# Block-sparse attention by query blocks of 32, 256 score columns a head, in front of a decoded-weight MLP

## The chip, the cores and the metric

The kernel runs on one core of one Trainium2 chip. The time is device microseconds of one execution. TensorE multiplies (PE in the profile, PEld its weight loads), VectorE (DVE), ScalarE (ACT) and GpSimd (POOL) do the element-wise work, and SyncE (SP) issues the transfers to 16 DMA engines.

## The reference

Attention over 4 batches, 8 heads, 768 positions and 64 dimensions, in blocks of 32; then a two-layer MLP on the 3,072 tokens of 512 features.

```python
scores = scale * np.matmul(q, k.transpose(0, 1, 3, 2))
mask = np.abs(blk_i - blk_j) <= window          # window = 1, blocks of 32, 24 of them
mask = mask | (blk_i == 0) | (blk_j == 0) | (blk_i == n_blocks - 1) | (blk_j == n_blocks - 1)
for qb in range(n_blocks):
    for kb in sampled_blocks[qb]:               # 3 drawn blocks per query block
        mask[qb * block:(qb + 1) * block, kb * block:(kb + 1) * block] = True
scores = np.where(mask, scores, -1000000000.0)
attn = np.exp(scores - np.max(scores, axis=-1, keepdims=True))
attn = attn / (np.sum(attn, axis=-1, keepdims=True) + 1e-09)
x = np.matmul(attn, v)                          # then [tokens, 512]
h = x @ w_in                                    # 512 x 2048
r = np.maximum(h, 0.0)
out = (s * (r * r) + b) @ w_out                 # 2048 x 512
```

So a query of an inner block sees its own block and both neighbours, the first and the last block, and three drawn ones: eight blocks, 256 keys, some of which coincide and are masked out. The queries of the first and of the last block see all 768 keys. q and k are 8 times larger than the draw above would give. The weights arrive as 64-bit floats.

## The kernel before

The attention part is cut into 52 slots, 26 for each pair of batches (pair 0 is batches a and b of the ORD strings, L26-33). Of the 26, 20 are s slots: 128 queries (four inner blocks, t = 0 to 4) of four heads (x = 0 or 1) of one batch. Two are h slots (t = 5, the remaining two inner blocks of all eight heads, packed as four units of 128 rows), and four are d slots, the dense queries of the first and last block. In pair 0 the d slots come first, in pair 1 last.

A slot's work goes through these steps. Its scores go to PSUM, one head per bank: `scores_static` (L878) multiplies 128 queries by 256 keys, which are six neighbouring blocks (own and neighbour blocks of all four query blocks) and the two outer blocks, read from `k_seq`, a layout of K that holds the outer blocks again between the others. `scores_sampled` (L904) adds 96 columns for the three drawn blocks of each query block, in tiles of 64 x 32, from `kg`, into which GpSimd copies the drawn blocks (L838). VectorE adds the mask and finds the maximum over 352 columns (L919), ScalarE exponentiates (L931), TensorE transposes three pieces of 128 x 128 per head (L955), and VectorE or ScalarE copies them out (L959, L961), one copy per head. TensorE then multiplies by the values: `av_static` (L1000) two pieces of 128 keys by 64 columns, from `v_sta`, and `av_sampled` (L1014) the drawn ones from `vg`, which is filled block by block by indexed loads on SyncE's queue (L821). The result is scaled (L1020), transposed (L1026), copied (L1031) and written to a scratch tensor in DRAM, `xd` (L1043). The result and its transpose live in one PSUM bank of their own, so a slot's values begin when the slot before has been copied out. d slots have their own code (L892 scores, L989 values).

Weights: each 128 x 512 block of `w_in` (i0 to i15) and `w_out` (o0 to o15) is loaded raw (L57) and turned by `decode_f64` into a high and a low part, on VectorE in six steps (L75, L77, L78, L83, L84, L85) and ScalarE in three. The MLP of batch 0 then runs as a first layer `mlp1` (L404-406: high x high, high x low, low x high), relu (L409), square (L416), high and low part of the hidden values (L420, L421, L425), and a second layer `mlp2` (L446-448). Its input is read back from `xd` (L364) and split into two parts (L377 on ScalarE, L379 on VectorE). The later batches use sums of blocks in seven products (L583).

The order on every engine is fixed before the run by the class `Plan`, a list scheduler: each operation has an engine, a modelled cost, a due number counted in units (heads), what it depends on and which rotating buffer it takes. At each step the operation that can start first by the model is put next on its engine. TensorE's attention order is tied by hand: transposes of slot i, the transpose of x of slot i-1, scores of slot i+2, values of slot i. The table T (L26-33) holds how many units ahead loads stand (KL for K, GK for the copies of drawn keys, GV for drawn values, VL for values), and the order of the decodes (WL).

Of the kernel before, what the change touches and what calls it, by code (L numbers as in the profile page):

```python
# [9 lines left out]
F32 = mybir.dt.float32  # L10
F32R = mybir.dt.float32r
# [191 lines left out]
def kernel(  # L203
# [26 lines left out]
    KW = k_seq.shape[-1]  # L230
    SC = 256
    SW = SC + NSL * BLK
# [23 lines left out]
    def kbig(q, name):  # L256
        return kp.tile([P, NPAIR, KW], F32R, tag=f"kt{q}", name=name, bufs=1)

# [9 lines left out]
    gp = ctx.enter_context(tc.tile_pool(name="gp", bufs=4))  # L268
# [25 lines left out]
    def win(f, part):  # L294

        return win_tile(f // 4)[:, (4 * part + f % 4) * NW:(4 * part + f % 4 + 1) * NW]

    def win_tile(k):
        if k not in wts:
            wts[k] = kbig(k, f"win{k}").rearrange("p a c -> p (a c)")  # L300
        return wts[k]
# [58 lines left out]
    xsp, xraw = {}, {}  # L360
# [6 lines left out]
    def xsplit(g, c, part=None):  # L367
# [5 lines left out]
        for k in range(2) if part is None else (part,):  # L373
            if c == 0:
                xsp[(g, k)] = gp.tile([P, NCC, HALF], F32R, tag="kg", name=f"x{g}_{k}")
# [108 lines left out]
    def ready_rest():  # L484
# [3 lines left out]
        spare = [win_tile(k)[:, 8 * NW:8 * NW + HN] for k in range(4)]  # L488
# [29 lines left out]
    def xplace(n):  # L518
        if n not in xop:
            t = gp.tile([P, 2 * HX], F32R, tag="kg", name=f"x{n}")  # L520
            xop[n] = t[:, :HX], t[:, HX:]
        return xop[n]
# [104 lines left out]
    with ExitStack() as es:  # L627
# [3 lines left out]
        vp = es.enter_context(tc.tile_pool(name="vp", bufs=4))  # L631
# [23 lines left out]
        def load_k(b, p):  # L655
            if p == 0:
                kts[b] = kbig(b, f"kt{b}").bitcast(F32)
            nc.sync.dma_start(out=kts[b][:, p, :], in_=k_seq[b, p])

        qraw, vst = {}, {}  # L660
# [10 lines left out]
        def load_v(i, pr):  # L671
            kind, b, t, x = slots[i]
            vt = vp.tile([P, NCH, P], F32, tag="v", name=f"v{i}_{pr}")
            if kind == "d":
                h0 = (2 * x + pr) * P
                nc.sync.dma_start(out=vt, in_=v[b, :, h0:h0 + P].rearrange("(c p) d -> p c d", p=P))
            elif kind == "h":
                vt = vt.rearrange("p c d -> p (c d)")[:, :8 * D]
                nc.sync.dma_start(out=vt.rearrange("p (x d) -> p x d", x=2), in_=v_edge[b].rearrange("x p d -> p x d"))
            else:  # L680
                vt = vt.rearrange("p c d -> p (c d)")[:, :8 * D].rearrange("p (c d) -> p c d", c=2)
                nc.sync.dma_start(out=vt, in_=v_sta[b, t, x])
            vst[(i, pr)] = vt

# [9 lines left out]
        for t in ptiles:  # L694
            nc.gpsimd.memset(t[:, SW:], 0.0)

# [26 lines left out]
        def sampled_blocks():  # L723
# [3 lines left out]
        mh = pers.tile([P, 2 * P], BF16, name="mh")  # L727
        kidx = pers.tile([P, (4 * NSP + 2) * NSL], I32, name="kidx")
        vidx = pers.tile([P, (4 * NSP + 2) * NSL], I32, name="vidx")


        wm = pers.tile([P, 6], F32, name="wm")
        V.tensor_scalar(out=wm, in0=jf[:, :6], scalar1=rf, scalar2=-1.0, op0=ALU.subtract, op1=ALU.add)
        V.tensor_tensor(out=wm, in0=wm, in1=wm, op=ALU.mult)
        V.tensor_scalar(out=wm, in0=wm, scalar1=1.0, scalar2=NEG, op0=ALU.is_gt, op1=ALU.mult)
        nc.gpsimd.memset(ms[:, :, P:P + 2 * BLK], 0.0)
        nc.scalar.copy(ms[:, :, :P].rearrange("p t (c e) -> p t c e", e=BLK),
                       wm[:, :4].unsqueeze(1).unsqueeze(3).broadcast_to([P, NSP, 4, BLK]))
        nc.scalar.copy(ms[:, :, P + 2 * BLK:SC].rearrange("p t (c e) -> p t c e", e=BLK),
# [715 lines left out]
```

## Time and profile before

| what | value |
|---|---|
| median of three runs | 802.29 us (799.03 to 805.81) |
| the profiled execution, its span | 803.1 us |
| first score matmul (a d slot) | 11.2 us |
| values of the first s slot | 47.75 us |
| last copy of transposed weights / last values of attention | 281.4 / 283.4 us |
| first matmul of the second layer | 297.6 us |

The profile is of one execution of 803.1 us, 0.1% above the median. Engine shares are shares of that span. In the rows of a stretch, busy time of each engine stands with the number of instructions in brackets, then the clock that TensorE was granted (1.00 is full speed), the busy share of the 16 DMA engines, and GB/s. In rows of time the first number is the start, the second the duration, x the number of instructions in a row; fp32 matmuls leave two records each. The bracket at the end gives idle time ahead and what ended it.

### The profile page before, as it was taken

The page shows a single profiled execution, that of the slowest core. Times are in us where ns is not written, and L with a number is a line of the kernel's source. Part 1 is how long each engine was busy: PE and PEld are TensorE (multiplying, and loading weights), DVE is VectorE, ACT ScalarE, POOL GpSimd, SP SyncE. Part 2 cuts the span into 40 slices and gives each one's busy share as a digit, 9 for nine tenths or more (in the row PEclk, how much of TensorE's full clock was granted, in tenths as well). Part 3 has the DMA queues.
Part 4 walks back from the last instruction along what each step waited for, and adds up shares of the span by engine and source line. Part 5 has one row for each costly group of instructions (what it writes and reads, how often), then busy time and mean ns, then how long its engine had stood idle before and what let it go on. Part 6 is the DMA issues. An engine that isn't in the chain of part 4 may idle for free.

```text
span 803.1 us, 22021 instructions
## 1 busy us (share of the span) xinstructions
PE 777.3 (97%) x8352; PEld 674.1 (84%) x8352; DVE 606.0 (75%) x1528; ACT 501.7 (62%) x1190; POOL 178.2 (22%) x404
## 2 busy tenths in 40 slices
PE   7898999899999999999998999999999999999997
PEld 6587877788877798999987999998888988999986
DVE  5476768788888898998789678678667768766662
ACT  3576768688787877778875443467355457544542
POOL 5422124222400000000003322233223223222321
PEclk9899999999999999999999999999999999999999
DMA  9998898877778532544332222024000012000002
GB/s 251 244 233 306 222 260 221 252 199 210 207 218 267 167 112 79 184 158 131 131 118 93 79 101 91 27 86 156 3 0 1 1 40 98 1 1 1 1 0 79
DMA packets 89001, 100.99 MB, mean 126 GB/s; under 512 B 11584, under 2 KB 66368, under 8 KB 88896
## 3 DMA queue, kind: packets, MB, share of 16 engines
q1 hardware_dynamic: 88896, 99.59, 41.2%
q8 instruction: 66, 1.08, 0.6%
q14 instruction: 39, 0.32, 0.1%
HBM read 80.68 MB, written 14.68 MB: 119 GB/s over the span
## 4 chain that ended last, share of the span: by engine, by line
PE 83%; DVE 5%; DMA 4%; ACT 3%; SPq 2%; issue 2%; ACTq 0%; DVEq 0%
PE m L583 19%; PE o L447 10%; PE o L448 10%; PE o L446 10%; PE t L955 8%; PE xs L1000 5%; PE s L878 5%; PE xs L1014 3%; PE h L404 3%; PE h L406 3%; PE h L405 3%; DMA kt<-in_k_seq_dram 2%; PE s L904 2%; PE xs L989 1%; PE s L892 1%
## 5 line engine op out<-in xcount | busy, mean ns | idle before, releaser
L425 POOL TENSOR_TENSOR hid<-hid,hid 128x384 fp32r<-128x384 f32 x96 | 106.1, 1106 | 468.5 <-ACT hid L601 457.3
L600 ACT ACTIVATE hid<-hid,sb_b,sb_s 128x384 f32<-128x384 f32 x96 | 68.0, 709 | 151.7 <-DVE hid L594 151.6
L931 ACT ACTIVATE ptile<-ptile,nm 128x352 f32<-128x352 f32 (+2 forms) x208 | 121.0, 584 | 33.8 <-DVE nm L919 33.2
L919 DVE CUSTOM_DVE_ANT_0 ptile<-s,ms 128x352 f32<-128x352 f32 x160 | 74.3, 521 | 29.0 <-PE s L904 28.5
L838 POOL COPY kg<-kt 128x128 f32 x264 | 64.1, 297 | 138.8 <-PE s L904 126.2
L955 PE MATMUL t<-ident,ptile 128*128 128x128 f32 x608 | 80.0, 281 | 4.7 <-ACT ptile L931 3.1
L583 PE MATMUL m<-wout,win 128*128 128x384 f32 x384 | 83.5, 338 | 1.0 <-ACT xrest L1348 1.0
L448 PE MATMUL o<-woutr,hid 128*128 128x512 f32 x192 | 75.9, 395 | 0.0
L447 PE MATMUL o<-woutr,hid 128*128 128x512 f32 x192 | 75.8, 395 | 0.0
L955 PEld LDWEIGHTS t<-ident,ptile 128*128 128x128 f32 x608 | 66.7, 142 | 10.5 <-ACT ptile L931 4.0
L446 PE MATMUL o<-woutr,hid 128*128 128x512 f32 x192 | 74.6, 389 | 0.0
L583 PEld LDWEIGHTS m<-wout,win 128*128 128x128 f32 x384 | 68.9, 188 | 4.9 <-ACT xrest L1348 1.4
L959 DVE COPY pt<-t 128x384 f32<-128x384 f32 (+1 forms) x104 | 56.2, 544 | 8.9 <-PE t L955 7.1
L961 ACT COPY pt<-t 128x384 f32<-128x384 f32 (+1 forms) x104 | 48.3, 474 | 17.6 <-PE t L955 16.7
L583 PE MATMUL m<-xT,wop 128*128 128x384 f32 x288 | 58.3, 337 | 0.0
L594 DVE SCALAR_TENSOR_TENSOR hid<-hid 128x384 f32<-128x384 f32 x96 | 54.5, 568 | 3.3
L601 ACT CAST hid<-hid 128x384 fp32r<-128x384 f32 x96 | 49.3, 514 | 7.8 <-PE o L448 0.4
L583 PEld LDWEIGHTS m<-xT,wop 128*128 128x128 f32 x288 | 51.5, 188 | 2.1
L593 DVE TENSOR_TENSOR hid<-m,xrest 128x384 f32<-128x384 f32 x48 | 26.5, 552 | 30.2 <-issue 25.6
L1000 PE MATMUL xs<-v,pt 128*64 128x64 f32 x1280 | 46.5, 225 | 2.1 <-issue 2.1
L1000 PEld LDWEIGHTS xs<-v,pt 128*64 128x64 f32 x1280 | 40.7, 138 | 9.0 <-issue 2.3
L448 PE MATMUL o<-wout,hid 128*128 128x512 f32 x120 | 47.4, 395 | 0.0
(186 smaller groups left out, 1759.6 us busy)
## 6 DMA issues: line engine op xcount, KB each, us to landing
vg<-in_v_dram SPq DMA_DIRECT2D x136, 128.0 KB, 3.6
v<-in_v_sta_dram SPq DMA_DIRECT2D x40, 256.0 KB, 4.4
kt<-in_k_seq_dram SPq DMA_DIRECT2D x16, 544.0 KB, 8.1
raw_i<-in_w_in_dram SPq DMA_DIRECT2D x16, 512.0 KB, 4.9
raw_o<-in_w_out_dram SPq DMA_DIRECT2D x16, 512.0 KB, 3.3
v<-in_v_dram SPq DMA_DIRECT2D x16, 384.0 KB, 7.1
xd<-xst SPq DMA_DIRECT2D x44, 128.0 KB, 3.4
out_dram<-ob SPq DMA_DIRECT2D x20, 256.0 KB, 2.0
```

Source lines behind the costliest of these rows:

```text
L425: (eng or nc.vector).tensor_tensor(out=htile(5 + i % 3), in0=t, in1=gh.bitcast(F32), op=ALU.subtract)
L446: nc.tensor.matmul(acc, gh[:, tsl], wout(f, 0), start=first, stop=False)
L447: nc.tensor.matmul(acc, gh[:, tsl], wout(f, 1), start=False, stop=False)
L448: nc.tensor.matmul(acc, gl[:, tsl], wout(f, 0), start=False, stop=last)
L583: nc.tensor.matmul(to, w_, x_, start=(c == 0 and k == 0), stop=(c == 1 and k == 2))
L600: nc.scalar.activation(t, t, AF.Identity, bias=sb_b, scale=sb_s)
L838: nc.gpsimd.tensor_copy(kg[:, m], kts[b][:, :, bass.ds(box["js"][m], BLK)])
L919: nc.vector.tensor_tensor_reduce(out=pt[:, :w], in0=sps.pop((n, g))[:, :w], in1=msk, scale=-scale, scalar=FMAX if g == 0 else nm[:, 0:1], ...
L931: nc.scalar.activation(pt[:, :w], pt[:, :w], AF.Exp, bias=nms[n][:, last:last + 1], scale=-1.0, accum_out=dns[i][:, g, j:j + 1])
L955: nc.tensor.transpose(tp[:, c, :], src[:, c * P:(c + 1) * P], ident)
L959: nc.vector.tensor_copy(to, src)
L1000: nc.tensor.matmul(xs[rows], pt[:, c, rows], vt[:, c, hp * D:(hp + 1) * D], start=(j == 0 and c == 0), stop=False, skip_group_check=True)
```

## The change

Every inner query block now gets its own eight blocks of keys and nothing more: 256 score columns for each head instead of 352. The columns are the own block and its neighbours (0 to 95, `OWN`), one outer block (96 to 127), the three drawn blocks (128 to 223, `SAM`), the other outer block (224 to 255). All scores of s and h slots come from `scores_piece`, in tiles of 64 x 32 (one per query block, head and piece); both kinds of slot run the same code. Values come from `av` in tiles of 128 x 32, with 128 keys each: the own window with the first block, and the drawn blocks with the last block. Two heads share a PSUM bank, in the scores (two banks a slot instead of four) and in the transposes (four pieces of 128 x 128 in a bank, copied out together, one copy on VectorE and one on ScalarE).

For this K is loaded by pairs of batches from `k_blk`, block by block, in four parts of 786,432 bytes, and any score of the pair waits for all four. `kg` holds the drawn keys of both batches (two buffers instead of four, each twice as large; half as many copies, twice as wide). The values of an s slot are loaded as windows: for each of its four query blocks the 96 rows around it, from `v`, into one of four fixed places `vw` (by batch of the pair and x), whose last 32 rows hold the first block, loaded once for a batch and half. `vg` gets the last block in its last 32 rows. The buffers for values of d and h slots fall from four to three. Decoded `w_in` blocks lie in other places (six in each K tile, four in the `vw` places). The split x lies in the `kg` buffers. Three masks and an index table are no longer built. In T, GK goes from 9 to 13, VL from 10 to 12, and KL has one entry for each pair.

```diff
-    "GK": 9.0, "GV": [9.0, 15.0, 15.0, 15.0, 15.0, 15.0], "KL": [26.0, 18.0, 26.0, 26.0], "QL": 18.0, "VL": 10.0, "SI": -30.0, "MS1": -30.0, "MS2": -29.0,
+    "GK": 13.0, "GV": [9.0, 15.0, 15.0, 15.0, 15.0, 15.0], "KL": [26.0, 40.0], "QL": 18.0, "VL": 12.0, "SI": -30.0, "MS1": -30.0, "MS2": -29.0,
...
-    SC = 256
-    SW = SC + NSL * BLK
+    SW = 256
+    OWN, SAM = 0, 4 * BLK
...
-    gp = ctx.enter_context(tc.tile_pool(name="gp", bufs=4))
+    gp = ctx.enter_context(tc.tile_pool(name="gp", bufs=2))
...
-        return win_tile(f // 4)[:, (4 * part + f % 4) * NW:(4 * part + f % 4 + 1) * NW]
+        k, n = (f // 6, 2 * (f % 6) + part) if f < 12 else (f - 10, part)
+        return win_tile(k)[:, n * NW:(n + 1) * NW]
...
-        vp = es.enter_context(tc.tile_pool(name="vp", bufs=4))
+        vp = es.enter_context(tc.tile_pool(name="vp", bufs=3))
...
-            nc.sync.dma_start(out=kts[b][:, p, :], in_=k_seq[b, p])
+            rows = slice(part * NB // KP, (part + 1) * NB // KP)
+            nc.sync.dma_start(out=kts[e][:, rows].rearrange("p n a c -> p n (a c)"),
+                              in_=k_blk[rows, :, 2 * e:2 * e + 2, :].rearrange("n p a c -> p n (a c)"))
...
-                nc.sync.dma_start(out=vt, in_=v_sta[b, t, x])
+                vt = window_place(b, x)
+                nc.sync.dma_start(out=vt[:NSL * BLK], in_=window_rows(b, 4 * t, 4, x * DM // 2, DM // 2))
...
+        def window_rows(b, first, n, d0, nd):
+            return bass.AP(v.tensor, v.offset + (b * S + first * BLK) * DM + d0, [[DM, NSL * BLK], [BLK * DM, n], [1, nd]])
...
+        def load_first_block(b, x):
+            nc.sync.dma_start(out=window_place(b, x)[NSL * BLK:],
+                              in_=v[b, :BLK, x * DM // 2:(x + 1) * DM // 2].unsqueeze(1).broadcast_to([BLK, 4, DM // 2]))
...
-                nc.gpsimd.tensor_copy(kg[:, m], kts[b][:, :, bass.ds(box["js"][m], BLK)])
+                nc.gpsimd.tensor_copy(kg[:, m:m + 1].rearrange("p o a c -> p o (a c)"),
+                                      kts[e][:, bass.ds(box["js"][m], 1)].rearrange("p o a c -> p o (a c)"))
...
+        def scores_piece(i, k, keys_of, o, n, two=False):
+            qr, u = qraw[slots[i][:3]], unit_of[i]
+            for par in range(2):
+                to = sps[(u + 2 * k + par, 0)][:, o:o + n]
+                if two:
+                    to = sps[(u + 2 * k + par, 0)].rearrange("p (a c) -> p a c", a=2)[:, :, o:o + n]
+                for r in range(4):
+                    pair, m, block = part_of(i, k, r)
+                    rows = slice(r * BLK, (r + 1) * BLK)
+                    nc.tensor.matmul(to[rows], qr[halves[par], pair, rows], keys_of(halves[par], pair, m, block),
+                                     start=True, stop=True, tile_position=(par * D, r * BLK))
...
+            scores_piece(i, k, lambda rows, pair, m, block: keys(b, rows, slice(block - 1, block + 2), pair), OWN, NSL * BLK)
+            scores_piece(i, k, lambda rows, pair, m, block: keys(b, rows, slice(0, NB, NB - 1), pair), NSL * BLK, BLK, True)
...
+            for j in range(1 if dense else 2):
+                src = pbuf[(n + j, g)]
+                for c in range(3 if dense else 2):
+                    nc.tensor.transpose(tp[:, (2 * j + c) * P:(2 * j + c + 1) * P], src[:, c * P:(c + 1) * P], ident)
...
+                    values = vg[:, b % 2, m, (h0 + h) * D:(h0 + h + 1) * D] if c else own[:, m, h * D:(h + 1) * D]
+                    nc.tensor.matmul(xs[rows], pt[:, c, rows], values, start=(j == 0 and c == 0), stop=(c == 1),
                                      tile_position=(0, r * BLK), skip_group_check=True)
```

What this makes of TensorE's rows in one s slot of batch 0, from its scores to its neighbour's values. Before (xs is the result, pt the transposed weights, x4 four matmuls alike):

```order
L878 MATMUL s_2663<-kt_184,qr_3s 128x256
L878 MATMUL s_2665<-kt_184,qr_3s 128x256
L878 MATMUL s_2675<-kt_184,qr_3s 128x256
L878 MATMUL s_2677<-kt_184,qr_3s 128x256
L904 MATMUL s_2663<-kg_3_1651,qr_3s 32x96 x4
L904 MATMUL s_2665<-kg_3_1651,qr_3s 32x96 x4
L904 MATMUL s_2675<-kg_3_1651,qr_3s 32x96 x4
L904 MATMUL s_2677<-kg_3_1651,qr_3s 32x96 x4
L1000 MATMUL xs_2702<-v_0_2238,pt_0_2657 64x64 x4
```

And in the new order, on the same engine at the same place (the first and second row are the own blocks, the third and fourth the outer ones):

```order
L920 MATMUL s_2268<-kt_149,qr_3s 32x96 x4
L920 MATMUL s_2269<-kt_149,qr_3s 32x96 x4
L920 MATMUL s_2268<-kt_149,qr_3s 32x2x32 x4
L920 MATMUL s_2269<-kt_149,qr_3s 32x2x32 x4
L920 MATMUL s_2268<-kt_149,qr_3s 32x96 x4
L920 MATMUL s_2269<-kt_149,qr_3s 32x96 x4
L920 MATMUL s_2268<-kt_149,qr_3s 32x2x32 x4
L920 MATMUL s_2269<-kt_149,qr_3s 32x2x32 x4
L920 MATMUL s_2268<-kg_3_1627,qr_3s 32x96 x4
L920 MATMUL s_2269<-kg_3_1627,qr_3s 32x96 x4
```

Four wide matmuls for 256 columns have become 32 small ones for 160 columns, and two banks (s_2268, s_2269) hold what four held.

The second place is VectorE at the seam between attention and MLP, around the decode of o0 (raw_o0 into the first `wout`). Before, i7 is the last block of w_in ahead of it:

```order
L83 TENSOR_TENSOR win1_5743<-wkhp1_3159,raw_i7_6287 128x512
L84 TENSOR_SCALAR wkhp1_3159<-win1_5743 128x512
L425 TENSOR_TENSOR hid5_7084<-hid0_7046,hid2_7069 128x384
L416 SCALAR_TENSOR_TENSOR hid1_7080<-hid1_7080,sb_s_62 128x384
L85 SCALAR_TENSOR_TENSOR win1_5743<-wklp1_3180,wkhp1_3159 128x512
L416 SCALAR_TENSOR_TENSOR hid0_7046<-hid0_7046,sb_s_62 128x384
L77 TENSOR_SCALAR wklp0_3179<-raw_o0_6663 128x512
L425 TENSOR_TENSOR hid6_7115<-hid1_7080,hid3_7100 128x384
L78 SCALAR_TENSOR_TENSOR wklp0_3179<-wklp0_3179,raw_o0_6663 128x512
```

In the new order, on VectorE behind the last squares of that stretch:

```order
L75 TENSOR_SCALAR wkhp1_4890<-raw_i6_7252 128x512
L83 TENSOR_TENSOR win0_5451<-wkhp0_4889,raw_i5_7242 128x512
L84 TENSOR_SCALAR wkhp0_4889<-win0_5451 128x512
L85 SCALAR_TENSOR_TENSOR win0_5451<-wklp0_4903,wkhp0_4889 128x512
L77 TENSOR_SCALAR wklp1_4904<-raw_i6_7252 128x512
L78 SCALAR_TENSOR_TENSOR wklp1_4904<-wklp1_4904,raw_i6_7252 128x512
L83 TENSOR_TENSOR win1_7393<-wkhp1_4890,raw_i6_7252 128x512
L84 TENSOR_SCALAR wkhp1_4890<-win1_7393 128x512
L85 SCALAR_TENSOR_TENSOR win1_7393<-wklp1_4904,wkhp1_4890 128x512
L75 TENSOR_SCALAR wkhp1_4890<-raw_i7_7367 128x512
```

The decodes of i3 to i7 now stand between the last copy of attention and o0, where before those of i6 and i7 stood; and all eight VectorE splits of the x of batch 0 (L390), of which before one was left, stand there too.

The third place is SyncE's queue near the end of attention. Before, raw_i6, raw_i7 and raw_o0 are issued among the loads of d slots (v48, v49):

```order
L57 DMA raw_i6_6265<-in_w_in_dram 128x4x256
L57 DMA raw_i7_6287<-in_w_in_dram 128x4x256
L682 DMA v47_0_6293<-in_v_sta_dram 128x512
L364 DMA wout1_6301<-xd_68 128x3x256 x2
L1043 DMA xd_68<-xst43_6334 128x256
L676 DMA v48_0_6403<-in_v_dram 128x6x128
```

In the new order, raw_i4 comes only behind the last loads of values (v51) and the last part of the x of batch 0 (xraw0_1):

```order
L1070 DMA xd_68<-xst49_7110 128x2x64
L697 DMA v51_1_7146<-in_v_dram 128x6x128
L375 DMA xraw0_1_7150<-xd_68 128x3x256
L1070 DMA xd_68<-xst50_7183 128x2x64
L57 DMA raw_i4_7235<-in_w_in_dram 128x4x256
```

Loads of weights have moved behind the loads of values; those up to raw_i3 stand a few rows earlier.

More of the change, by code (lines that the diff above doesn't have):

```diff
@@ L868, with scores_dense @@
         halves = [slice(par * D, (par + 1) * D) for par in range(2)]
+        def scores_dense(i, k):
+            kind, b, t, x = slots[i]
+            n, qr = unit_of[i], qraw[slots[i][:3]]
+            for par in range(2):
+                sp = sps[(n + par, k)] = next_bank(f"s{n + par}_{k}")
+                for a in range(2):
+                    nc.tensor.matmul(sp[halves[a], :HALF], qr[halves[par], 2 * x + a, halves[a]],
+                                     keys(b, halves[par], slice(k * NB // 2, (k + 1) * NB // 2), 2 * x + a),
+                                     start=True, stop=True, tile_position=(par * D, a * D))
@@ L898, in scores_sampled @@
             for k in range(2):
[L899 to L906 removed]
+                scores_piece(i, k, lambda rows, pair, m, block: kg[rows, m * NSL:(m + 1) * NSL, b % 2, pair * BLK:(pair + 1) * BLK],
+                             SAM, NSL * BLK)
```

351 lines of the change are left out of this document (169 added, 182 removed).

## The prediction

> **What bounds the kernel now.** I read the page's busy table and slices first, then busy time by stage, then one attention slot on TensorE, then the seam between attention and the MLP on VectorE.
>
> The page: span, busy shares, and the slices of DMA share and bandwidth (40 slices of 20 us).
>
> ```profile
> span 803.1 us, 22021 instructions
> PE 777.3 (97%) x8352; PEld 674.1 (84%) x8352; DVE 606.0 (75%) x1528; ACT 501.7 (62%) x1190; POOL 178.2 (22%) x404
> DMA  9998898877778532544332222024000012000002
> GB/s 251 244 233 306 222 260 221 252 199 210 207 218 267 167 112 79 184 158 131 131 118 93 79 101 91 27 86 156 3 0 1 1 40 98 1 1 1 1 0 79
> ```
>
> TensorE is busy 97% of the span. The transfers fill the first eight slices at 0.8 and more of the 16 DMA engines and ease later. So during attention two resources are near their limits. Busy time by stage says how near (the last three columns: granted TensorE clock, DMA share, GB/s):
>
> ```profile
> core 0: us, PE busy (x) PEld busy (x) DVE busy (x) ACT busy (x) POOL busy (x), PEclk, DMA share, GB/s
> 0.00:40.00 40.00, 30.53 (x335) 22.93 (x335) 20.58 (x80) 17.31 (x50) 19.53 (x92) 0.87 0.93 248
> 40.00:80.00 40.00, 37.94 (x876) 31.15 (x876) 27.17 (x97) 27.93 (x86) 11.65 (x48) 1.00 0.91 269
> 36.00:160.00 124.00, 117.18 (x2772) 96.02 (x2771) 89.27 (x320) 88.71 (x269) 36.71 (x153) 0.99 0.87 247
> 160.00:250.00 90.00, 89.64 (x2175) 73.63 (x2174) 75.61 (x263) 71.99 (x218) 18.75 (x78) 1.00 0.74 210
> ```
>
> From 160 to 250 TensorE never stops (89.6 of 90 us), and from 36 to 160 it is busy for 117.2 of 124 us with the DMA engines at 0.87. From slice 28 on the transfers nearly stop, and the MLP is left to TensorE. One s slot (four heads, 128 queries) on TensorE, as start, duration and work:
>
> ```profile
> 161.30 1.14 PE L878 MATMUL s<-kt,qr_0s 64*128 64x256 f32 x8
> 162.36 0.56 PE L904 MATMUL s<-kg,qr_0s 64*32 64x96 f32 x32
> 162.85 1.15 PE L1000 MATMUL xs<-v,pt 128*64 128x64 f32 x32
> 163.94 0.65 PE L1014 MATMUL xs<-vg,pt 96*32 96x64 f32 x32
> 164.52 1.53 PE L955 MATMUL t<-ident,ptile 128*128 128x128 f32 x12
> 165.89 0.38 PE L1026 MATMUL xs<-ident,xss 128*128 128x128 f32 x2
> 166.20 1.13 PE L878 MATMUL s<-kt,qr_0s 64*128 64x256 f32 x8
> ```
>
> From start to start the pieces are 1.06, 0.49, 1.09, 0.58, 1.37 and 0.31 us: 4.90 us a slot, and there are 40 such slots.
>
> **The change on TensorE.** A matmul of the source stands as two records, so x32 is 16 matmuls.
> - Scores: the 4 wide matmuls (1.06 us) go. In their place come 16 of 64x32 by 96 columns, the very shape of L904 (0.49 us), and 16 of 64x32 by 64 columns. The trace has no such row with 64 columns; its price lies between 64/96 of 0.49 = 0.33 and the whole 0.49. I take 0.42. With the sampled ones, unchanged at 0.49, scores cost 1.40 against 1.55 us.
> - Values: the 16 + 16 matmuls (1.09 + 0.58) become 32 of 128x32 by 64 columns. L1014 has this form with 96 rows instead of 128: 2 x 0.58 = 1.16 us, 0.51 less.
> - Transposes: 8 instead of 12, 8/12 of 1.37 = 0.91 us. The transposes of x stay at 0.31.
> - Sum: 1.40 + 1.16 + 0.91 + 0.31 = 3.78 us, 1.12 less; over 40 s slots 44.8 us. The four h slots get the same work as an s slot where they had a smaller one; I take +0.2 us each, so 44 us net. The d slots keep their matmuls.
>
> The softmax becomes narrower on the other two engines:
>
> ```profile
> L931 ACT ACTIVATE ptile<-ptile,nm 128x352 f32<-128x352 f32 x160 | 93.4, 585 | 15.5 <-DVE nm L919 15.0
> L931 ACT ACTIVATE ptile<-ptile,nm 128x256 f32<-128x256 f32 x16 | 8.1, 505 | 0.8 <-DVE nm L919 0.8
> L919 DVE CUSTOM_DVE_ANT_0 ptile<-s,ms 128x352 f32<-128x352 f32 x160 | 74.3, 521 | 29.0 <-PE s L904 28.5
> L919 DVE CUSTOM_DVE_ANT_0 ptile<-s,mh 128x256 f32<-128x256 f32 x16 | 5.8, 421 | 2.3 <-PE s L904 2.2
> L959 DVE COPY pt<-t 128x384 f32<-128x384 f32 x96 | 52.9, 555 | 8.8 <-PE t L955 7.1
> L961 ACT COPY pt<-t 128x384 f32<-128x384 f32 x96 | 45.5, 482 | 17.3 <-PE t L955 16.4 <-ACT x L377 0.6
> ```
>
> Per s slot ScalarE saves 4 x 0.080 in exponentials, and one copy of 512 columns (4/3 of 0.482, at most 0.64) takes the place of two (0.96): 0.64 us off a slot in which it is busy for 0.80 x 4.90 = 3.92. VectorE saves 4 x 0.100 and about 1.11 - 0.74, so 0.77 off 0.84 x 4.90 = 4.12. Both come to 3.3 us, under 3.78, so neither is the bound: I cost them at nothing, covered by the matmuls. GpSimd's gather copies halve in number and double in width; it is busy for 37 of 124 us, and its copies stand 13 units ahead instead of 9. Nothing either.
>
> **The change on the DMA queue.** These rows give the sizes that are issued now:
>
> ```profile
> vg<-in_v_dram SPq DMA_DIRECT2D x136, 128.0 KB, 3.6
> v<-in_v_sta_dram SPq DMA_DIRECT2D x40, 256.0 KB, 4.4
> kt<-in_k_seq_dram SPq DMA_DIRECT2D x16, 544.0 KB, 8.1
> ```
>
> K falls from 16 x 544 KB = 8.9 MB to 8 x 786,432 B = 6.3 MB. The values of an s slot are now the three blocks around each of four query blocks, 96 rows x 4 x 1 KB = 393 KB instead of 262: 40 x 131 KB = +5.2 MB, and with the first-block loads +6.3. The h windows add 1.0, and the last block beside the sampled values about 0.5. In all attention issues 68.8 MB instead of 64.6. A steady s slot costs 1,048 KB (sampled values 393, window 393, q 131, spill 131) instead of 917. At the 4.90 us of now, 917 KB is 187 GB/s; at 3.78 us, 1,048 KB would be 277 GB/s, and K of the second pair and the first weights come on top. The busiest long stretches of the trace carry 247, 248 and 269 GB/s at shares of 0.87 to 0.93; scaled to a full share that is 267 to 296. So the cover that the slower matmuls gave the transfers is gone: what is late next is the window or sampled-value load.
>
> Counted along SyncE's rows in the new order, 11.1 MB stand ahead of the first s slot's values and 62.1 MB up to the last s slot's window. The first part takes 11.1/0.248 = 45 us from about 2 us on, so 47. That is where these values stand today, which leaves nothing lost at the start:
>
> ```profile
> 47.75 1.15 PE L1000 MATMUL xs<-v,pt 128*64 128x64 f32 x32
> ```
>
> The remaining 51 MB take 189 us at 270 GB/s, which I choose because the stretch nearest to the new load (40 to 80 us, both q and windows flowing) shows 269; the ends are 206 us at 248 and 179 at 285. So the last window is there at about 236 us. Today the last s slot's values start at 266.2 us and the last values of attention end at 283.4, which is 17 us for the d slots:
>
> ```profile
> 266.16 0.65 PE L1014 MATMUL xs<-vg,pt 96*32 96x64 f32 x32
> 281.80 1.62 PE L989 MATMUL xs<-v,pt 128*64 128x64 f32 x48
> ```
>
> So attention ends near 252 to 253, 31 us earlier, of the 44 that TensorE alone would give.
>
> The Trainium skill, "DMA: Bandwidth & Descriptors" (Specifications; Where 436 GB/s comes from) puts the HBM limit of a core at about 358 GB/s. By it the 51 MB would take an estimated 142 us and never bind, and the sum would be that of the first rival. The rows above speak against it: 0.93 of the engines' time carried 248.
>
> **The change at the seam.** Before the first second-layer matmul, VectorE must decode weight block o0. Its order is fixed. Now, after the last copies of attention, it decodes i6 and i7, does one split of x, and then o0:
>
> ```profile
> 280.23 1.17 DVE L959 COPY pt<-t 128x384 f32<-128x384 f32 x2
> 281.59 0.54 DVE L379 TENSOR_TENSOR x<-wout,x 128x384 fp32r<-128x384 f32 x1
> 296.01 0.69 DVE L85 SCALAR_TENSOR_TENSOR wout<-wklp,wkhp 128x512 fp32r<-128x512 f32 x1
> 297.22 0.69 DVE L83 TENSOR_TENSOR wout<-wkhp,raw_o 128x512 fp32r<-128x512 f32 x1
> ...
> 299.01 0.42 DVE L75 TENSOR_SCALAR wkhp<-raw_o 128x512 int32<-128x512 int32 x1
> 299.35 0.42 DVE L77 TENSOR_SCALAR wklp<-raw_o 128x512 int32<-128x512 int32 x1
> 299.80 0.69 DVE L78 SCALAR_TENSOR_TENSOR wklp<-wklp,raw_o 128x512 f32<-128x512 int32 x1
> 297.64 0.39 PE L446 MATMUL o<-wout,hid 128*128 128x512 f32 x1
> ```
>
> A decode is six steps (L75, L77, L78, L83, L84, L85). Six in a row stand from 297.22 to the end of L78 at 300.49: 3.2 us without the overlap with the next. A split (L379) is about 0.5. Today o0 is done at 296.7, 15.3 us after the last copy (281.4), and the matmul starts at 297.6. In the new order five decodes (i3 to i7) and eight splits stand there: three decodes and seven splits more, 3 x 3.2 + 7 x 0.5 = 13.1, less 0.8 for two steps of o1 that stand ahead of it today and no longer will: +12 us. TensorE has seven first-layer blocks to do meanwhile in either order; today they fill the 14 us from 283.4 to 297.6, so it will idle for most of those 12. The lower end is nothing, if ScalarE's steps and the loads, not VectorE, release o0 today; the upper end is +15, if the raw loads, which will stand behind the last spills, come late. I take +12, since VectorE's own steps alone fill the time to 296.7. After so long a wait TensorE runs at the low clock:
>
> ```profile
> 142.76 0.61 PE L1014 MATMUL xs<-vg,pt 96*32 96x64 f32 x26 [2.39 <-DMA vg<-in_v_dram]
> 143.30 2.27 PE L955 MATMUL t<-ident,ptile 128*128 128x128 f32 x12
> 145.93 1.81 PE L878 MATMUL s<-kt,qr_4s 64*128 64x256 f32 x8
> ```
>
> After 2.39 us of waiting, L955 took 2.27 instead of 1.53 and L878 1.81 instead of 1.14: 1.4 us lost. I add 1.4 once, and 1 us for d-slot values, whose buffers fall from 4 to 3.
>
> **Sum.** 803.1 - 31 + 12 + 1.4 + 1 = 786.5 for the profiled execution; the median of the runs is 802.3, 0.8 below it, so 786.
>
> **Rivals.**
> - The transfers keep pace (285 GB/s and more), and TensorE paces attention: 44 us off instead of 31, 786 - 13 = 773. For it: the slice with 306 GB/s. Against it: no stretch of 40 us passes 269.
> - The transfers hold only the 248 GB/s of the first 40 us: 51 MB take 206 us, attention ends 17 us later than forecast, 803, no change. For it: the new loads of windows are 1 KB pieces instead of 2 KB. Against it: 40 to 80 us.
> - Slower: each wait on a late load puts TensorE at the low clock, and the slot behind it costs 1.4 us more, as at 143.30. By the forecast the average slot waits about 0.9 us. From 12 such slots on the gain is gone (786 + 12 x 1.4 = 803), from 18 on it is over 1% slower; with 20 it gives 814. For it: the row at 143.30, and the clock of 0.87 in the first 40 us. Against it: from 40 to 80 us, with DMA at 0.91, the clock stays at 1.00; and waits get fewer where a slow slot lets the queue catch up. The Trainium skill, "TensorE: Matmul & The Clock Gate" (Part 1), ties the low clock to an idle window of about 3.4 us; by that rule short waits would not trip it, and the row above, tripped by 2.39 us, reads otherwise.
>
> **Chances.** Forecast 0.49, keeps pace 0.19, 248 GB/s 0.22, low clock 0.10. A measurement of this kernel tells about 1% (8 us) from no change. The first two lie below 794: faster 0.68. The third is within 1%: 0.22. Slower 0.10. The range runs from 768 (keeping pace, with edge scores at 0.33) to 806 (248 GB/s, and two low-clock slots); above and below about 0.15 is left out.
>
> **What would show it.** An s slot on TensorE of 3.7 to 3.9 us where nothing is late; DMA share 0.9 or more from 40 to 230 us, with TensorE waiting on windows or sampled values; last values of attention at 252; some 10 us of idle TensorE ahead of the first second-layer matmul, released by VectorE's wout; nothing moved later. Wrong: no waits on transfers (then 773), a clock under 0.9 through attention (then 803 and up), or no idle at the seam.

## The result and the profile after

The changed kernel takes 881.1 us (four runs, 880.7 to 883.1) against 803.3 before: 1.0985 times as long (95% interval 1.0947 to 1.1023). 786 was forecast, with a range to 806. From the page of the changed kernel, span, busy shares, granted clock and DMA share by slices of 22 us, and the queue that carries instructions (packets, MB, share of the DMA engines):

```profile
span 879.1 us, 26215 instructions
PE 763.2 (87%) x10688; PEld 665.7 (76%) x10688; DVE 572.4 (65%) x1476; ACT 475.8 (54%) x1144; POOL 159.8 (18%) x266
PEclk8899898898899989899999999999999999999999
DMA  9996666798676946436434322212400001100001
q8 instruction: 84, 1.38, 0.7%
```

The same queue in the kernel before:

```profile
q8 instruction: 66, 1.08, 0.6%
```

TensorE does less work (763 us busy, not 777) in 2,336 more matmul records, and no compute engine is near its limit in attention. The time by stage, from the first and last rows of each:

| stage | before | after | difference |
|---|---|---|---|
| to the first drawn values | 48.8 | 53.1 | +4.3 |
| s and h slots, to the end of the last drawn values | 218.0 | 273.3 | +55.4 |
| d slots, to the last transpose of x | 17.7 | 18.0 | +0.3 |
| to the first second-layer matmul | 13.1 | 26.6 | +13.5 |
| the rest | 505.5 | 508.0 | +2.6 |

Busy time of the changed kernel in the last four stages (d slots and seam in one row; stretch, length, busy time by engine, clock, DMA share, GB/s):

```profile
53.12:326.46 273.34, 193.28 (x7215) 161.21 (x7211) 127.91 (x533) 132.37 (x440) 38.13 (x108) 0.88 0.74 196
326.46:371.07 44.61, 31.21 (x362) 27.26 (x362) 39.52 (x97) 32.96 (x75) 0.00 (x0) 0.93 0.50 146
371.07:879.10 508.03, 500.85 (x2460) 448.03 (x2460) 381.67 (x758) 288.96 (x565) 105.48 (x96) 0.99 0.21 68
```

and the slots of the kernel before:

```profile
48.84:266.81 217.97, 209.78 (x5014) 171.11 (x5012) 170.46 (x600) 165.51 (x499) 49.65 (x204) 0.99 0.81 233
```

In the slots TensorE is busy for 193 instead of 210 us, but idle for 80 instead of 8, at a clock of 0.88, with the DMA engines at 0.74. What it waits for over the whole span, the changed kernel's longest (total, times, longest):

```profile
PE xs L1041 <- issue: 34.7, 15, 4.3
PE s L920 <- issue: 24.5, 20, 2.8
PE t L993 <- issue: 11.9, 6, 4.2
PE o L457 <- DVE wout L83: 10.5, 1, 10.5
PE xs L1026 <- DMA v<-in_v_dram: 7.5, 2, 5.9
PE s L900 <- DMA qr_5d<-in_q_edge_dram: 4.6, 1, 4.6
PE xs L1041 <- DMA vg<-in_v_dram: 4.5, 2, 3.6
```

The rows of L1026 and L900 are d slots ahead of the stage; within the slots the loads of values (vg, and v of an h slot) cost 7.0 us of waiting. "Issue" is idle time for which the profile shows no releaser. There are 42 such waits over 0.1 us between 53 and 310 us, 72.8 us in all; the kernel before has three, 3.6 us. They fall in the middle of runs of like matmuls, and their places give the cause away. In TensorE's order of time (start, duration, work, wait):

```profile
107.34 0.38 PE L920 MATMUL s<-kt,qr_2s 64*32 64x96 f32 x16 [0.15 <-issue]
111.45 0.49 PE L993 MATMUL t<-ident,ptile 128*128 128x128 f32 x3 [1.44 <-issue]
...
181.67 0.52 PE L920 MATMUL s<-kg,qr_0s 64*32 64x96 f32 x19 [2.78 <-issue]
187.13 0.39 PE L920 MATMUL s<-kt,qr_0s 64*32 64x96 f32 x17 [2.12 <-issue]
192.62 0.88 PE L993 MATMUL t<-ident,ptile 128*128 128x128 f32 x6 [1.71 <-issue]
```

Between 107.34 and 111.45 stand 127 matmul records, from 181.67 on 127 and 128; through the whole stage the waits lie 125 to 128 records apart or a multiple of that (253 to 256, 381). A record has a weight load beside it, so 128 records are 256 instructions. The instruction queue says the same: 1.38 MB in 84 packets is 16.4 KB each, and 21,376 matmul and load records divided by 256 are 83.5; before, 16,704 by 256 are 65.3, and 66 packets. TensorE gets its program in blocks of 256 instructions, one packet each, and now runs dry at the end of a block. The trace has these packets one by one, and they settle it: every one of the 42 waits ends 1.2 to 1.7 us behind the landing of a packet. The packet ahead of 187.13, for one, starts at 184.60 and lands at 185.92. A block came every 4.1 us near 107 us and every 5.5 near 185. The stretches around them differ in the DMA share, 0.60 and 0.93 (same columns as above):

```profile
80.00:120.00 40.00, 31.20 (x1209) 26.52 (x1213) 18.57 (x79) 19.03 (x65) 6.29 (x18) 0.87 0.60 174
...
160.00:200.00 40.00, 24.58 (x851) 20.31 (x849) 14.96 (x67) 16.00 (x56) 4.17 (x12) 0.84 0.93 222
```

A slot of the changed kernel has 80 matmuls of two records and ten transposes of one (the rows of L993 and L1053), 170 records with as many weight loads: 340 instructions. Before it had 118 records, 236 instructions, in 4.90 us. The expectations below count a transpose as two records, and so 20 instructions a slot too many for forms of the changed kernel (360, 312, 216) and 28 too many for the kernel before (264, 312, 376).

The Trainium skill, "Runtime: NRT & Kernel Launch" (Instruction fetch mechanics), describes these blocks of 16 KiB and 256 instructions, and calls the cost of crossing from one to the next mostly hidden. This trace agrees on the size and not on the cost.

Where nothing is late, a slot takes about what was forecast (3.78). The changed kernel has two such slots at full clock, each from one transpose of x to the next:

```profile
102.24 0.38 PE L1053 MATMUL xs<-ident,xss 128*128 128x128 f32 x2
106.13 0.38 PE L1053 MATMUL xs<-ident,xss 128*128 128x128 f32 x2
...
201.32 0.38 PE L1053 MATMUL xs<-ident,xss 128*128 128x128 f32 x2
...
204.89 0.38 PE L1053 MATMUL xs<-ident,xss 128*128 128x128 f32 x2
```

They take 3.89 and 3.57 us. 44 of the longer one are 171 us; the busy time is 193. The other 22 us are, by my estimate, the low clock: 0.88 of 193 is 170.

### The profile page after: what moved, and what is told of

Read it like the earlier page. It is cut to its first block, busy times and chain, and to the rows that moved or that the text cites. A ratio compares the mean times of both kernels' runs of the same rounds, so it can differ in the third digit from the quotient of the medians.

```text
span 879.1 us, 26215 instructions
## 1 busy us (share of the span) xinstructions
PE 763.2 (87%) x10688; PEld 665.7 (76%) x10688; DVE 572.4 (65%) x1476; ACT 475.8 (54%) x1144; POOL 159.8 (18%) x266
## 3 DMA queue, kind: packets, MB, share of 16 engines
q8 instruction: 84, 1.38, 0.7%
## 4 chain that ended last, share of the span: by engine, by line
PE 76%; issue 9%; DVE 6%; DMA 4%; ACT 3%; SPq 1%; ACTq 0%; DVEq 0%
PE m L594 18%; PE o L458 9%; PE o L459 9%; PE o L457 9%; PE t L993 7%; PE s L920 7%; PE xs L1041 6%; DMA v<-in_v_dram 2%; PE h L416 2%; PE h L417 2%; PE h L415 2%; PE xs L1053 1%; PE s L900 1%; DMA kt<-in_k_blk_dram 1%; PE xs L1026 1%
## 5 line engine op out<-in xcount | busy, mean ns | idle before, releaser
L968 ACT ACTIVATE ptile<-ptile,nm 128x256 f32<-128x256 f32 (+1 forms) x208 | 107.9, 520 | 66.8 <-DVE nm L956 66.8
L956 DVE CUSTOM_DVE_ANT_0 ptile<-s,ms 128x256 f32<-128x256 f32 x160 | 58.3, 421 | 78.9 <-PE s L920 78.9
L993 PE MATMUL t<-ident,ptile 128*128 128x128 f32 x448 | 74.1, 317 | 12.0 <-issue 11.9
L1041 PE MATMUL xs<-vg,pt 128*32 128x64 f32 x1408 | 54.8, 236 | 34.1 <-issue 27.1
L860 POOL COPY kg<-kt 128x256 f32 x132 | 46.4, 404 | 207.3 <-PE s L920 194.0
L1006 ACT COPY pt<-t 128x512 f32<-128x512 f32 (+1 forms) x60 | 33.3, 557 | 84.9 <-PE t L993 83.2
L993 PEld LDWEIGHTS t<-ident,ptile 128*128 128x128 f32 x448 | 58.2, 162 | 19.9 <-issue 15.4
L1041 PEld LDWEIGHTS xs<-vg,pt 128*32 128x32 f32 x1408 | 42.1, 120 | 36.6 <-issue 31.7
L594 PE MATMUL m<-xp,wop 128*128 128x384 f32 x288 | 58.3, 337 | 0.0
L457 PE MATMUL o<-wout,hid 128*128 128x512 f32 x120 | 48.3, 402 | 10.7 <-DVE wout L83 10.5
L594 PE MATMUL m<-xp,win 128*128 128x384 f32 x288 | 55.7, 340 | 1.4 <-DVE xp L578 0.7
L594 PEld LDWEIGHTS m<-xp,win 128*128 128x128 f32 x288 | 51.4, 189 | 4.3 <-DVE xp L578 1.2
L1041 PE MATMUL xs<-vw,pt 128*32 128x64 f32 x1280 | 47.8, 238 | 7.6 <-issue 7.6
```

Source lines behind the costliest of these rows:

```text
L457: nc.tensor.matmul(acc, gh[:, tsl], wout(f, 0), start=first, stop=False)
L594: nc.tensor.matmul(to, w_, x_, start=(c == 0 and k == 0), stop=(c == 1 and k == 2))
L956: nc.vector.tensor_tensor_reduce(out=pt[:, :w], in0=sps.pop((n, g))[:, :w], in1=msk, scale=-scale, scalar=FMAX if g == 0 else nm[:, 0:1], ...
L968: nc.scalar.activation(pt[:, :w], pt[:, :w], AF.Exp, bias=nms[n][:, last:last + 1], scale=-1.0, accum_out=dns[i][:, g, j:j + 1])
L993: nc.tensor.transpose(tp[:, (2 * j + c) * P:(2 * j + c + 1) * P], src[:, c * P:(c + 1) * P], ident)
L1041: nc.tensor.matmul(xs[rows], pt[:, c, rows], values, start=(j == 0 and c == 0), stop=(c == 1), tile_position=(0, r * BLK), skip_group_chec ...
```

## The experiments

Theory S: instructions come too late, so what counts is how many a slot has. R1: late values, as the prediction had it. R2: the small tiles themselves.

**Fewer instructions for the outer blocks (edge_wide).** The outer keys are the same for all four query blocks.

```diff
-            scores_piece(i, k, lambda rows, pair, m, block: keys(b, rows, slice(0, NB, NB - 1), pair), NSL * BLK, BLK, True)
+            m = 1 if kind == "s" else 2
+            for par in range(2):
+                to = sps[(n + 2 * k + par, 0)].rearrange("p (a c) -> p a c", a=2)[:, :, NSL * BLK:P]
+                for r in range(m):
+                    pair = 2 * x + k if kind == "s" else 2 * k + r
+                    rows = slice(r * P // m, (r + 1) * P // m)
+                    nc.tensor.matmul(to[rows], qraw[slots[i][:3]][halves[par], pair, rows],
+                                     keys(b, halves[par], slice(0, NB, NB - 1), pair),
+                                     start=True, stop=True, tile_position=(par * D, r * P // m))
```

> The changed kernel, with the outer-block scores of an s slot as 4 matmuls of 64x128 by 64 columns instead of 16 of 64x32 (in h slots 8 of 64x64): TensorE instructions of an s slot 312 instead of 360, same loads. Theory S (TensorE's instructions arrive in blocks of 256, one 16 KB packet each, and attention waits for them): attention shortens by about 48/360 = 13% of its 230 us of s and h slots, so about 850 us, stalls still 128 matmul records apart. Rival R1 (late windows and drawn values, as predicted): nothing but noise, 881. Rival R2 (the array itself is slower with small tiles): only the array time of the 12 matmuls, 40 x 0.15 = 6 us, 875.

863.2 us, 1.0724 times before (1.067 to 1.0778); the slots take 255.1 us instead of 273.3. S gave 850: the direction is right, the size is short by 13. The waits for issue fell to 31 us, but an undisturbed slot grew to about 4.2 us; a run below says why.

**More instructions in the kernel before (before_split, before_more).** First each static score matmul in four tiles, then also in two halves (the second edit):

```diff
-                    nc.tensor.matmul(sp[:, :SC], qr[halves[par], 2 * x + k, :], kt[halves[par], 2 * x + k, 192 * t:192 * t + SC],
-                                     start=True, stop=True, tile_position=(par * D, 0))
+                    for r in range(4):
+                        rows = slice(r * BLK, (r + 1) * BLK)
+                        for c in range(2):
+                            nc.tensor.matmul(sp[rows, c * P:(c + 1) * P], qr[halves[par], 2 * x + k, rows],
+                                             kt[halves[par], 2 * x + k, 192 * t + c * P:192 * t + (c + 1) * P],
+                                             start=True, stop=True, tile_position=(par * D, r * BLK))
```

> The kernel before, with each static score matmul (128 queries by 256 keys) cut into four tiles of 64x32 over the same keys: same loads, same columns, TensorE instructions of an s slot 312 instead of 264. S: at the 4.1 to 5 us that a block of 256 took in the changed kernel a slot takes 5.0 to 6.1 us instead of 4.9, so 810 to 845 us, with stalls 128 records apart. R1: 803, as no load changes. R2: up to 10 us slower, without such stalls.

> The kernel before, with each static score matmul cut into eight pieces (four tiles of 64x32, two halves of 128 columns): loads, columns and everything behind the scores as before, TensorE instructions of an s slot 376 instead of 264 (360 in the changed kernel). If instructions alone suffice: a slot takes at least 376/256 x 3.47 = 5.1 us and, with the transfers of before beside it, up to the 6.2 of the changed kernel: 815 to 860 us, a block of 128 records late almost every time, clock near 0.95. If the changed kernel's slowness needs its larger loads: within 10 us of the 814 that the milder cut gave.

814.5 us (1.0165, 1.0089 to 1.0242) and 841.6 us (1.0462, 1.0384 to 1.054), with the same loads and columns; the first is clear of no change, though not of 2%. The slots go from 218.0 to 224.8 and 251.7 us; the second one's row:

```profile
49.15:300.88 251.73, 227.77 (x7087) 198.64 (x7084) 172.48 (x600) 165.63 (x498) 49.29 (x204) 0.99 0.69 202
```

Both are inside what S gave, and the larger loads of the changed kernel are not needed for it. The 34 us of the second one are not all instructions that came late: the waits for issue rise from 3.6 to 23 us, in 25 waits and not almost every time, and an undisturbed slot takes 5.15 instead of 4.90 us, some 10 us in 40 slots, which may be the small tiles themselves. The clock stayed at 0.99, not the 0.95 that was expected.

**The pace of a block by itself (flood, flood_slow).** 1,024 extra matmuls ahead of one product in the third product stage of the kernel before, 32 columns or 128:

```diff
+        if (p, s, n) == (3, 2, 1):
+            for y in range(1024):
+                r, par = y % 4, 0
+                nc.tensor.matmul(to[r * BLK:(r + 1) * BLK, :32], w[0][par * 64:(par + 1) * 64, r * BLK:(r + 1) * BLK].bitcast(F32),
+                                 xh[par * 64:(par + 1) * 64, :32].bitcast(F32), start=True, stop=True, tile_position=(par * 64, r * BLK))
```

> The kernel before with 1,024 extra matmuls of 64x32 by 32 columns (4,096 TensorE instructions, 16 blocks of 256) in the third product stage, where the DMA engines are idle; their results are overwritten. The array needs some 10 to 18 ns a record, 20 to 37 us in all. S with a fixed pace of 4 us a block: stalls at every 128 records and 55 to 65 us longer. S with contention: a block comes in 2 us or less, few or no stalls, 20 to 37 us longer. R2: no stalls 128 records apart.

> The 1,024 extra matmuls in the quiet stage with 128 columns each instead of 32: four times the columns for the same 4,096 instructions. S: 128 records now take the array longer than the 3.47 us that a block took, so no stalls there, and only 0 to 20 us longer than with 32 columns (862 to 882). If the pace were the array's: about four times the 59 us that the 32 columns cost, above 1,000.

With 32 columns 862.5 us (one run). In the stretch the clock is at 0.51 and the DMA engines are at 0.02:

```profile
589.00:645.00 56.00, 30.43 (x1825) 28.49 (x1826) 0.20 (x1) 0.57 (x2) 0.00 (x0) 0.51 0.02 4
```

```profile
601.23 1.93 PE L582 MATMUL m<-wout,win 64*32 64x32 f32 x128 [1.53 <-issue]
604.72 1.94 PE L582 MATMUL m<-wout,win 64*32 64x32 f32 x128 [1.55 <-issue]
608.20 1.93 PE L582 MATMUL m<-wout,win 64*32 64x32 f32 x128 [1.55 <-issue]
```

128 records, a wait of 1.5 us, again and again: a block every 3.46 to 3.49 us with nothing beside it, and from 618 us on every 3.74 to 4.02. (The low clock does not look like the reason: the shortest distance in after_quiet below, where its mean was 0.96, is 3.4 too.) With 128 columns, 865.4 us (one run), and this:

```profile
589.40 31.45 PE L582 MATMUL m<-wout,win 64*32 64x128 f32 x1128
621.15 25.34 PE L582 MATMUL m<-wout,win 64*32 64x128 f32 x896 [0.30 <-issue]
646.82 0.86 PE L582 MATMUL m<-wout,win 64*32 64x128 f32 x24 [0.32 <-issue]
```

Four times the columns for 3 us and no waits to speak of: the 59 us of the first run were the instructions. So 340 instructions take at least 340/256 x 3.48 = 4.6 us, where the slot of the kernel before took 4.90: even with empty queues the change could have kept only about 0.3 of the 1.12 us a slot that it was to save. Of S's two cases the fixed pace is the nearer one, at 3.48 us a block instead of 4.

Where the time of a block goes is read from the packets (us; from the end of one wait of TensorE to the end of the next):

| wait ends | until the next packet starts | its duration | from its landing to the end of the next wait |
|---|---|---|---|
| flood, 601.23 | 1.16 | 1.05 | 1.28 |
| changed kernel, 111.45 | 1.49 | 1.10 | 1.51 |
| changed kernel, 181.67 | 2.93 | 1.32 | 1.21 |
| changed kernel, 187.13 | 2.79 | 1.06 | 1.64 |

Behind none of these waits does the next packet start before TensorE has gone on. Beside heavy loads it starts later, 1.2 to 3.5 us behind the waits from 160 to 200 us against 1.1 to 1.2 in flood; once it moves it is hardly slower (0.9 to 1.6 us in the slots of the changed kernel, 0.9 to 1.4 in flood).

**Without most loads of values (after_quiet, edge_quiet, few_quiet), and with fewer instructions still (few_instr).** The quiet ones load the windows and the drawn values once, so that most slots use old values:

```diff
+                new = (b // 2, b % 2, x) not in vseen and b < 2
+                vseen.add((b // 2, b % 2, x))
                 vt = window_place(b, x)
-                nc.sync.dma_start(out=vt[:NSL * BLK], in_=window_rows(b, 4 * t, 4, x * DM // 2, DM // 2))
+                if new:
+                    nc.sync.dma_start(out=vt[:NSL * BLK], in_=window_rows(b, 4 * t, 4, x * DM // 2, DM // 2))
...
+                if n >= 2:
+                    return
```

On top of edge_wide, few_instr also makes the own and the drawn scores of s slots wide, so that most of these scores are not those wanted:

```diff
+        def scores_wide(i, k, keys_of, o):
+            qr, u = qraw[slots[i][:3]], unit_of[i]
+            for par in range(2):
+                pair, m, block = part_of(i, k, par)
+                nc.tensor.matmul(sps[(u + 2 * k + par, 0)][:, o:o + NSL * BLK], qr[halves[par], pair, :], keys_of(halves[par], pair, m, block),
+                                 start=True, stop=True, tile_position=(par * D, 0))
```

> The changed kernel without most of its loads of values in attention: the four window places are loaded once and the two buffers of drawn values once, so 28 MB of some 69 are left out and the attention of most slots uses old values. S, where a block of instructions is late because it queues with the data: stalls fall from 73 us to under 25 and the time to 780 to 810. S, where a block takes its 4 us whatever the data do: stalls stay above 55 us, time above 860. R1: no waits, 773.

> The kernel with wide outer-block scores, where the own and the drawn scores of an s slot are also 4 matmuls each of 64x128 by 96 columns instead of 16 of 64x32: all four query blocks of a head get the keys of one of them, so most scores are not those wanted. Same loads, same columns; TensorE instructions of an s slot 216 instead of 312 (360 in the changed kernel). S: blocks of 256 are no longer late, stalls 128 records apart under 10 us in all, the clock back above 0.97, and the transfers' pace left as the bound, 189 us for the slots instead of 273: 785 to 800. R1 (late values made the changed kernel slow): still above 850. R2 (tiles of 32 columns themselves): the values still have them, so above 840.

> The kernel of few instructions, also without most loads of values (28 MB left out, as before). S: the array alone is left, 3.5 to 3.9 us a slot, about 163 us for the slots instead of 218 before: 760 to 775. If something else than instructions and transfers holds the slots, they stay near 5 us and the time above 800.

> Wide outer-block scores (312 instructions an s slot) and the 28 MB of value loads left out. By blocks alone 312/256 x 3.47 = 4.2 us a slot, so 190 to 205 us for the slots, between the 182 of few instructions and the 231 of the changed kernel without those loads: 795 to 815.

Times: 841.7, 826.6, 790.0 and 821.1 us, the last two of one run each. By the pages 29 MB less are read in the quiet ones. What decides is the length of the slots' stage (us):

| instructions of an s slot | all loads | 29 MB left out |
|---|---|---|
| 340 | 273.3 | 231.0 |
| 292 | 255.1 | 213.1 |
| 196 | 218.6 | 182.1 |

Down a column instructions cost 55 and 49 us, across a row the loads cost 42, 42 and 37: two causes, nearly additive. after_quiet stands between the two cases that S was given: its waits are 53 us, and most of its blocks come 3.4 to 4.1 us apart. The block is slowed by the data, yet too slow without most of them. Late values alone (R1) are refuted by the 231 us; R2 by the undisturbed slots, which take no longer with all the small tiles (3.57 and 3.89) than without those of the scores (3.84 in few_quiet). edge_quiet missed by 6 us; its undisturbed slot is longer, 4.2 us.

With 196 instructions the DMA engines are as full as I had forecast, only slower. The row of few_instr and its waits in that stage, then the row of few_quiet:

```profile
50.74:269.38 218.64, 183.06 (x4487) 157.68 (x4484) 128.08 (x536) 133.00 (x443) 37.84 (x108) 0.95 0.97 241
PE xs L1062 <- issue: 19.0, 12, 3.8
PE xs L1062 <- DMA vg<-in_v_dram: 11.5, 8, 3.9
PE s L920 <- issue: 5.1, 3, 1.9
```

```profile
53.19:235.27 182.08, 171.00 (x4487) 147.28 (x4484) 125.34 (x533) 131.28 (x440) 38.25 (x108) 0.99 0.47 133
```

At a share of 0.97 the engines carried 241 GB/s, not 270, and the slots take 218.6 us, as long as before. So with the instruction bound eased this layout still gains nothing in attention, and pays at the start and at the seam: 826.6, where S expected 785 to 800 by my rate. The waits for issue did not go under 10 us either: 24 remain, twice those for drawn values, beside transfers at that share. So late blocks and late values hold this version together.

**Where the wide tiles stand (edge_last).** All outer-block scores behind the slot's other scores, so that the tile shape changes once there and back instead of twice.

```diff
+            n = unit_of[i]
+            for k in range(2):
+                m = 1 if kind == "s" else 2
...
```

> Wide outer-block scores as in the run that gave 863, but all four behind the own and the drawn scores of the slot, so that TensorE goes from 64x32 to 64x128 tiles and back once a slot instead of twice. If the undisturbed slot of 4.2 us there (3.9 in the changed kernel, for more columns) is due to the changes of tile shape: 4.0 us a slot where nothing is late, and up to 10 us off, 853 to 860. If it is the wide matmuls themselves: 863 again. Theory S gives no other number, as the instructions are the same.

860.6 us (1.0732, 1.0668 to 1.0796), not to be told from 863.2. An undisturbed slot did shrink, to 3.86 us, and the next one met this:

```profile
105.83 0.43 PE L1063 MATMUL xs<-ident,xss 128*128 128x128 f32 x2
...
109.69 0.44 PE L1063 MATMUL xs<-ident,xss 128*128 128x128 f32 x2
...
111.46 0.45 PE L920 MATMUL s<-kt,qr_3s 64*32 64x96 f32 x20 [1.03 <-issue]
```

The waits for issue rose from 31 to 52 us: the array's gain went into waiting, as is to be expected where instructions set the pace. The second change of tile shape there and back had cost about 0.3 us a slot.

**The seam (seam_edge).** edge_wide with o0 decoded behind i2.

```diff
-    "WL": "i0 i1 i2 i3 i4 i5 i6 i7 o0 o1 o2 o3 o4 o5 o6 i8 o7 i9 o8 i10 o9 i11 o10 i12 o11 i13 o12 i14 o13 i15 o14 o15", "WP": 22.5, "WS": 15.5, "XP": 85.9,
+    "WL": "i0 i1 i2 o0 i3 o1 i4 i5 o2 i6 o3 i7 o4 o5 o6 i8 o7 i9 o8 i10 o9 i11 o10 i12 o11 i13 o12 i14 o13 i15 o14 o15", "WP": 22.5, "WS": 15.5, "XP": 85.9,
```

> The kernel with wide outer-block scores (863) and the decodes in another order, o0 behind i2 and o1 behind i3: the first second-layer matmul no longer waits 10.5 us for o0. If that wait is the cost of the seam: 852 to 855. If VectorE is only behind by that much and TensorE waits elsewhere: 860 or more.

862.0 us against 863.2: nothing. The second layer starts 9.8 us behind the last transpose of x instead of 26.7, and what follows takes 522.8 instead of 509.0 us. Rows of edge_wide and of seam_edge from that matmul to the end:

```profile
354.19:863.20 509.01, 500.82 (x2460) 447.44 (x2460) 381.86 (x758) 289.01 (x565) 105.61 (x96) 0.99 0.20 68
```

```profile
336.77:859.60 522.83, 508.80 (x2497) 453.52 (x2496) 399.27 (x789) 299.06 (x584) 105.55 (x96) 0.99 0.21 70
```

The wait of 10.5 us for o0 is gone, and shorter ones, none over 1.7 us, have come in behind. So the seam's price is not the place of o0; VectorE's backlog of decodes, which stays, is the reading that is left.

## Why the prediction was wrong

- **The step that failed** is "so neither is the bound", with what follows from it: the slot was weighed against the array, ScalarE, VectorE, GpSimd and the transfers, but not against TensorE's own instructions. Four wide matmuls became 32 small ones, and only their columns were priced. The row that could have told was on the page: 66 instruction packets for 16,704 TensorE records, one for each 256. The slot of before used one block in 5.3 us (236 instructions in 4.90), the forecast one in 2.8 (340 in 3.78), and flood got none faster than every 3.46. So TensorE waited 72.8 us for blocks.
- **TensorE's work** was right: 3.78 us forecast, 3.57 and 3.89 measured in undisturbed slots, 3.86 with wide edges placed last. That VectorE, ScalarE and GpSimd stay covered was right too: in the slots TensorE waits 0.3 us for them.
- **The transfers** were mis-sized: 270 GB/s taken, 241 measured at 0.97 of the engines once instructions were few; the 51 MB then take 218.6 us with their waits, not 189. That was the second rival, with its 248. With this term alone the forecast would have been "no gain". The parts listed for the added loads come to +5.2 MB, not the 4.2 between 64.6 and 68.8; by the pages 6.3 MB more are read. The forecast does not use that total.
- **The start** was put at no loss and cost 4.3 us: the first score comes at 14.1 instead of 11.2 us, and the d slots' values wait for their loads.
- **The seam**, forecast at +12 plus 1.4, measured +13.5 and +2.6 behind it. The mechanism fits VectorE's backlog, as worked out, with TensorE idle for 10.5 us ahead of o0; the remedy that it suggested does nothing.
- **The slower rival** named the low clock, and its price is there: 22 us at 0.88. Late data can be little of its cause, for TensorE waited only 7.0 us for values in the slots; what stands beside it is the waits for blocks. Flood shows the low clock, 0.51, with the DMA engines at 0.02 and nothing but such waits between small matmuls, and flood_slow, almost without the waits, 1.00; but the cut kernel of before, with 23 us of them, kept 0.99. How much waiting it takes is not shown. The row at 142.76 that priced this rival was not a single short wait either: 0.80 us of idle time end at 140.10, so that TensorE was idle for most of 3.5 us.

Together: 39 us less at full clock in the slots (210 to 171, an estimate), 22 for the clock and 72 for more idle time, 55 us in all; with start, d slots, seam and rest, 76 us of span.

No version with all the loads beats the kernel before (few_quiet, at 790.0, lacks 29 MB of them). Under load a block is late mainly because its packet starts later, hardly because it moves more slowly; with the 29 MB left out the median of that delay falls from 2.0 us to 1.3. That the packet queues behind data fits this, but no row shows it.

## What to carry to other kernels

When a change cuts matmuls into smaller ones, count TensorE's instructions a microsecond as a resource beside columns and bytes: fp32 matmuls are two weight loads and two multiplies each in these traces, transposes one of each, and here 256 instructions took 3.5 to 4 us with idle queues and mostly 4 to 6 beside heavy loads. The sign of it is idle time with no releaser in the middle of like matmuls, at even distances in records, each ending just behind the landing of an instruction packet. Where it binds, a faster array buys only longer waits; fewer, wider instructions or fewer bytes do help.

## What the runs showed of the hardware that was not expected

- 256 TensorE instructions arrived every 3.46 to 4.02 us with the DMA engines idle (flood), every 4.1 at a share near 0.6 and every 5.5 at 0.93 (changed kernel, near 107 and 185 us). What grows is the time until the packet starts, from 1.1 to as much as 3.5 us.
- 16 DMA engines at 0.97 carried 241 GB/s, 44 of 52 MB in pieces of 1 and 2 KB (few_instr).
- Going from 64x32 to 64x128 tiles and back twice a slot instead of once cost about 0.3 us (4.2 in edge_wide against 3.86 in edge_last).
